# Batch 0 routed in two parts, two experts in TensorE's column halves, and gate logits out of the matmul that turns rows back

## The chip, the cores and the metric

The kernel runs on one core of one Trainium2 chip. The core has five engines with an instruction stream each: TensorE (PE in the rows; PEld is its weight load), VectorE (DVE), ScalarE (ACT), GpSimd (POOL) and SyncE (SP), which here only issues DMAs. The metric is the device time of one execution in microseconds (us), lower is better. One profiled execution stands behind all rows.

## The reference, cut to what matters

```python
# q, k, v: (4 batches, 8 heads, 576 tokens, 64)
scores = q @ k.T / sqrt(64)
kth    = the 32nd largest score of each row
attn   = softmax(scores where scores >= kth, else -1e9)
x      = (attn @ v), heads side by side          # (2304 tokens, 512)
noisy  = x @ w_gate + log1p(exp(x @ w_noise)) * noise   # (2304, 8 experts)
top2, weights = two largest of noisy, softmax over the two
out[t] = sum over the two experts: weight * (relu(x[t] @ w1[e]) @ w2[e])   # 512 -> 1024 -> 512
```

So there is a sparse attention whose thirty-second largest score must be found in each row, a gate that sends each token to two of eight experts, and the experts' two layers.

## The kernel before

**Attention** is done in 144 units of 128 score rows by 576 keys, 36 to a batch: four pairs of heads, nine units to a pair (`attend`, `finish`). For a unit PE makes the scores, DVE folds and searches them (`fold`, `top8`, `drop8`, lines 648 to 666), POOL subtracts the mask (line 739), ACT takes the exponential (line 687), PE turns the result (lines 762 and 766). After each fourth unit `gather` multiplies with the values (lines 824 to 836), lifts the product (849), turns it back into rows of tokens (`back`, line 853, a transpose against the identity `ident`) and writes it to the row buffer `xr` (`out_`, 859 and 861). DVE and POOL later divide by the softmax sums (`norm`).

**Gate.** Once a pair of heads is done, `gate` turns its 128 columns of all five token tiles again (lines 930 and 933), ACT copies them, and five matmuls with the gate weights `wg` (line 944) give the logits, which are summed over the four pairs. `route`, once a batch, makes the top two, the place of each token in its experts' lists, and ten indirect DMAs from POOL (`xg<-xr,si`, line 1125), which scatter the rows into the experts' slots `xg`.

**Experts** run in groups of slots (`experts`, table `GROUPS`): after batch 0 all eight experts take 128 slots each, after batches 1 and 2 come further groups, after batch 3 the last. In groups of 128 slots a piece is `up1` (eight float32 matmuls of 128 columns, line 1315) or half of `down1` (one of 512 columns, line 1342); four `up1` and eight halves make an expert. The groups of 256 slots split every number into a high and a low part and use three matmuls for one (lines 1284 to 1286 and 1350 to 1352). Gathered rows are first turned (line 1250). SP loads weights ahead (`wr`).

**Order.** Nothing is ordered by the engines at run time: `Plan` simulates the five engines when the program is built and writes each engine's instructions out in the order that its cost table and priorities (`prio`, `PACE`, `WHEN` and others) give. Each engine then runs its list strictly in order and waits by semaphore. Where PE would be idle before the first expert rows are turned, `Plan.fill` puts fillers in (`filler`, lines 572 to 576: matmuls whose result nobody reads). `qkv` loads the queries, keys and values of a head; SP issues its DMAs in list order too.

Of the kernel before, what the change touches and what calls it, by code (L numbers as in the profile page):

```python
# [34 lines left out]
SIGNS = (10, 10, 8, 5)  # L35


WEIGHS = (700, 2400, 2100, 3400)
BIAS = (2000, 500, 500, 500)
BELOW = (1100, -3100, 2200, 4500)  # L40
LOWK = (2300, 1900, 500, 2600)
OUTS = (300, -100, 300, 300)
NORM = (3000, 400, -100, -1700)
LOWS = (2100, 1600, 2700)
LOWN = 13


def spread(i, tenths):
# [6 lines left out]
LOADS = (3, 6)  # L55
# [10 lines left out]
DROPS = (4, 0, 2, 0)  # L66

TAKE = ((0, 208), (48, HS), (0, HS))
GLAG = 1

SGAP, SLOT = (1500, 1600, 1600, 1500), (1, 1, 1, 1)

WHEN = (16, 13, -21, -12)
# [7 lines left out]
NT = 5  # L81

NE2 = 4
# [4 lines left out]
PACE = [(70, 54), (910, 40), (110, 23), (300, 18), (0, 0)]  # L88


class Node:
    __slots__ = ("eng", "dur", "fn", "deps", "users", "prio", "left", "ready", "lat", "start", "n", "share", "move", "bank", "alt", "ready2", "shy", "lock", "gap")


class Plan:
# [13 lines left out]
    def add(self, eng, dur, fn, deps=(), prio=None, lat=0, share=1.0, move=0, bank=False, alt=None, lock=False, gap=None):  # L109
# [5 lines left out]
        x.shy, x.lock, x.gap = None, lock, gap  # L115
# [29 lines left out]
    def order(self):  # L145
# [13 lines left out]
        now = dict(free)  # L159

# [9 lines left out]
        while left:  # L170
# [21 lines left out]
            if x.lock:  # L192

                at = locked["DVE" if e == "POOL" else "POOL"]
                if at > t:
                    heapq.heappush(wait[e], (at, x.n, x))
                    continue
            if x.bank:
# [33 lines left out]
            if x.move:  # L232
                moved = end = max(end + 1000, moved) + x.move
            left -= 1
# [104 lines left out]
def general_path(tc, C, ident, qk, v, noise, w1, w2, out, dram):  # L339
# [5 lines left out]
    with ExitStack() as ctx:  # L345
# [57 lines left out]
        ps = ctx.enter_context(tc.tile_pool(name="gq", bufs=1, space=PSUM))  # L403
        with tc.For_i(0, N, 128) as r0:
# [11 lines left out]
            for c in range(4):  # L416
                nc.tensor.matmul(lg[:, 0], xt[:, c], C["wg"][:, c], start=(c == 0), stop=(c == 3))
# [32 lines left out]
def sparse_attention_moe(ctx: ExitStack, tc: tile.TileContext, qk, v, wg, aux, noise, w1, w2, out):  # L450
# [25 lines left out]
    ident = C["ident"] = cp.tile([128, 128], F32, name="ident")  # L476
    nc.vector.tensor_scalar(ident, jp, 0.0, None, op0=OP.is_equal)
    C["tri"] = cp.tile([128, 128], BF, name="tri")
# [10 lines left out]
    for b, lo, nt, es in GROUPS[:-1]:  # L489
        for e in es:  # L490
            ends.setdefault(("end", b), {})[e] = lo + 128 * nt
    for nm, at in ends.items():
        C[nm] = cp.tile([128, 8], F32, name=nm if isinstance(nm, str) else f"end{nm[1]}")
        e = 0
        while e < E:
# [3 lines left out]
            e += n  # L499
    zc = P["m"].tile([128, 2, XW], F32, name="xs", bufs=1)  # L500
# [14 lines left out]
    ENG = {"DVE": nc.vector, "POOL": nc.gpsimd}  # L515
    bank = P["acc"].tile([128, 512], F32, name="bank")
# [6 lines left out]
    QN = {}  # L523

    def qkv(n):
        b, h = divmod(n, H)

        def whole():
            hi[n] = P["hi"].tile([128, QW + KW], F32, name="hi", bufs=4)
            nc.sync.dma_start(hi[n][0:64], qk[b, h])  # L530
            vt[n] = P["v"].tile([128, 6, D], F32, name="vt", bufs=NV)
            nc.sync.dma_start(vt[n], v[b, h])

        if b < NATIVE:
            a = add("SP", 1000, whole, move=1330, lat=700)
            QN[n] = (a, a, a, pl.take("hi", 4, a), None, pl.take("v", NV, a))
            return

        def load():
# [3 lines left out]
            vt[n] = P["v"].tile([128, 6, D], F32, name="vt", bufs=NV)  # L543
            nc.sync.dma_start(vt[n], v[b, h])
# [13 lines left out]
        a = add("SP", 1500, load, move=2200, lat=2500)  # L558
        r, vv = pl.take("raw", 2, a), pl.take("v", NV, a)
# [4 lines left out]
        z = add("POOL", 1625, low_q, [x], alt=("DVE", 850, LOWK[b]), lock=True)  # L564
# [14 lines left out]
    def place(j):  # L579

        b, jj = divmod(j, 36)
        hp, tt = divmod(jj, 9)
# [952 lines left out]
```

## Time and profile before

| | us |
|---|---|
| median of 3 runs | 958.43 (958.23 to 958.78) |
| the profiled execution | 957.39 |
| its span, first to last instruction | 955.5 |

The span is 1.9 us shorter than the time of the same execution. The page counts PE as busy for 96% of the span, DVE for 70%, ACT, POOL for 69% each, with the TensorE clock granted at 0.99 of full speed in the mean. A busy PE is no proof that PE sets the end: the fillers count as busy too, and matmuls are pipelined, so that the mean duration of one matmul is longer than the distance from its start to the start of the next. The distance is what counts for a sum, and it is read from the timeline.

### The profile page before, as it was taken

To read this page: it belongs to the slowest core of one execution; us is meant where nothing else is said; L and a number is where in the kernel's file an instruction comes from. 1 tells how busy PE (TensorE), PEld (TensorE's weight loads), DVE (VectorE), ACT (ScalarE), POOL (GpSimd) and SP (SyncE) were. 2 spreads that over 40 slices of the span, in tenths; PEclk is the share of its full clock that TensorE was granted. 3 is DMA by queue.
4 is the path that set the end of the run, shared out by engine and by line. 5 is a ranking of instruction groups with operands and counts; after the bars stand their busy time and mean duration, and the time that the engine had idled before them with its cause. 6 is when DMAs were issued, how large, how long until landed. Compare 5 with 4: busy or idle time off the path is not lost.

```text
span 955.5 us, 18621 instructions
## 1 busy us (share of the span) xinstructions
PE 916.4 (96%) x6239; PEld 706.7 (74%) x6260; DVE 665.6 (70%) x2161; ACT 655.9 (69%) x1516; POOL 655.7 (69%) x840
## 2 busy tenths in 40 slices
PE   9999999999999899899999999999989999999992
PEld 4555566567777677777777877877889999999991
DVE  7999989998999999899998893773543222222220
ACT  4888888777987689788767675575556555555540
POOL 4666576873755787577687563249877988888871
PEclk9999999999999999999999999999999999999996
DMA  9364531236676677955959779567877787777731
GB/s 297 112 233 167 207 73 45 75 114 168 195 230 182 203 254 234 248 170 160 278 175 294 235 226 287 187 226 254 257 247 238 210 259 225 229 227 226 233 75 26
DMA packets 122251, 190.61 MB, mean 199 GB/s; under 512 B 8225, under 2 KB 69665, under 8 KB 122145
## 3 DMA queue, kind: packets, MB, share of 16 engines
q1 hardware_dynamic: 113440, 169.10, 55.6%
q0 software_dynamic: 8704, 20.22, 9.7%
q8 instruction: 51, 0.84, 0.4%
q14 instruction: 56, 0.45, 0.2%
HBM read 153.02 MB, written 36.27 MB: 198 GB/s over the span
## 4 chain that ended last, share of the span: by engine, by line
PE 76%; DMA 5%; POOL 5%; ACT 5%; DVE 4%; issue 3%; SPq 1%; POOLq 0%; DVEq 0%; ACTq 0%
PE bk L1342 9%; PE hps L1315 8%; PE pp L762 6%; PE bank L824 5%; PE hps L576 5%; PE bk L618 5%; PE hps L1284 5%; PE hps L1286 4%; PE hps L1285 4%; PE bk L614 4%; PE bk L1350 3%; PE bk L1351 3%; PE bk L1352 3%; DMA wr<-in_w_dram 2%; PE hps L1250 2%
## 5 line engine op out<-in xcount | busy, mean ns | idle before, releaser
L661 DVE MAX8 t8s<-cat 128x8 f32<-128x288 f32 (+3 forms) x576 | 265.7, 489 | 7.2 <-POOL cat L675 5.0
L739 POOL TENSOR_TENSOR ss<-ss,mk 128x576 f32<-128x576 f32 x143 | 186.0, 1304 | 76.8 <-ACT mk L729 60.5
L1200 POOL TENSOR_TENSOR wl<-wr,wh 128x1024 fp32r<-128x1024 f32 x77 | 188.1, 2479 | 33.7 <-ACT wh L1196 33.5
L666 DVE MATCH_REPLACE8 cat<-t8s,cat 128x240 f32<-128x240 f32 (+2 forms) x411 | 161.3, 395 | 0.0
L648 DVE TENSOR_TENSOR cat<-bk,ss 128x288 f32<-128x288 f32 x288 | 127.0, 444 | 27.8 <-ACT ss L626 27.7
L1294 DVE SCALAR_TENSOR_TENSOR hl<-hps,hh 128x256 fp32r<-128x256 f32 x96 | 40.6, 423 | 145.5 <-ACT hh L1290 134.2
L687 ACT ACTIVATE ss<-ss,nb 128x576 f32<-128x576 f32 x144 | 112.0, 778 | 27.5 <-POOL ss L739 21.6
L1196 ACT ACTIVATE wh<-wr 128x1024 fp32r<-128x1024 f32 x96 | 99.8, 1054 | 43.2 <-PE bk L1352 25.2
L1315 PEld LDWEIGHTS hps<-xh,wr 128*128 128x128 f32 x1024 | 120.7, 192 | 11.4 <-issue 5.0
L1315 PE MATMUL hps<-xh,wr 128*128 128x128 f32 x1024 | 125.2, 276 | 3.2 <-DMA wr<-in_w_dram 2.4
L1342 PE MATMUL bk<-wr,hh 128*128 128x512 f32 x256 | 127.2, 594 | 0.0
L626 ACT ACTIVATE ss<-bk 128x288 f32<-128x288 f32 x288 | 109.1, 412 | 22.9 <-PE bk L614 12.3
L1284 PE MATMUL hps<-xh,wh 128*128 128x256 f32 x384 | 111.1, 289 | 2.4 <-DVE hl L1294 2.4
L1286 PE MATMUL hps<-xh,wl 128*128 128x256 f32 x384 | 108.7, 283 | 0.4 <-POOL wl L1200 0.4
L1285 PE MATMUL hps<-xl,wh 128*128 128x256 f32 x384 | 108.5, 282 | 0.0
L729 ACT ACTIVATE mk<-ss,under 128x576 bf16<-128x576 f32 x118 | 91.5, 777 | 18.4 <-POOL under L725 13.7
L771 ACT ACTIVATE pt<-pp 128x512 f32<-128x512 f32 x144 | 86.1, 598 | 17.1 <-PE pp L762 16.0
L618 PE MATMUL bk<-hi 128*128 128x288 f32 x240 | 91.1, 389 | 2.9 <-POOL hi L556 1.3
L762 PE MATMUL pp<-ident,ss 128*128 128x128 f32 x576 | 89.5, 278 | 3.1 <-ACT ss L687 2.7
L762 PEld LDWEIGHTS pp<-ident,ss 128*128 128x128 f32 x576 | 66.2, 142 | 35.4 <-issue 10.2
L1370 POOL DMA_INDIRECT out_dram<-yo,tok x40 | 65.9, 1647 | 26.9 <-ACT yo L1366 16.5
L576 PE MATMUL hps<-dummy 128*128 128x512 bf16 x293 | 81.4, 388 | 2.0 <-DVE dummy L468 0.9
(159 smaller groups left out, 1901.7 us busy)
## 6 DMA issues: line engine op xcount, KB each, us to landing
wr<-in_w_dram SPq DMA_DIRECT2D x224, 512.0 KB
raw<-in_qk_dram SPq DMA_DIRECT2D x48, 320.0 KB
xg<-xs SPq DMA_DIRECT2D x16, 528.0 KB
xs<-xg SPq DMA_DIRECT2D x12, 528.0 KB
vt<-in_v_dram SPq DMA_DIRECT2D x32, 192.0 KB
out_dram<-xs SPq DMA_DIRECT2D x1, 5120.0 KB
xs<-xg SPq DMA_DIRECT2D x16, 264.0 KB
hi<-in_qk_dram SPq DMA_DIRECT2D x8, 320.0 KB
```

The costliest lines, as they stand in the source:

```text
L576: nc.tensor.matmul(ps, C["dummy"].to_broadcast([128, 128]), C["dummy"].to_broadcast([128, 512]), start=True, stop=True)
L618: nc.tensor.matmul(sp, lhs(n), rhs, start=(k == 0), stop=(k == 2 * len(heads) - 1))
L661: return lambda: nc.vector.max(t["t8"][:, r], t["cat"] if r == 3 else t["cat"][:, slice(*TAKE[r])])
L666: nc.vector.match_replace(g, t["t8"][:, r], g, NEG)
L739: ENG[eng].tensor_tensor(t["s"], t["s"], t["mk"], op=OP.subtract)
L762: nc.tensor.transpose(pp[:, c], t["s"][:, k0 + c * 128:k0 + (c + 1) * 128], ident)
L1200: return lambda eng: ENG[eng].tensor_tensor(WS[m][1][:, i], W[m][:, i], WS[m][0][:, i].bitcast(F32), op=OP.subtract)
L1284: nc.tensor.matmul(ps[:, :NN], ah, xh, start=(c == 0), stop=False)
L1285: nc.tensor.matmul(ps[:, :NN], ah, xl, start=False, stop=False)
L1286: nc.tensor.matmul(ps[:, :NN], al, xh, start=False, stop=(c == 3))
L1315: nc.tensor.matmul(ps[:, f * 128:(f + 1) * 128], w[:, 0, a:a + 128], X["h", e][:, c, :128], start=(c == 0), stop=(c == 3))
L1342: nc.tensor.matmul(Y[e][0], HN["h", ff // 2][:, f * 128:(f + 1) * 128], W[4 * e + ff // 2][:, 1, f * 512:(f + 1) * 512], start=(ff == 0), ...
```

## The change

Four things change.

1. **Batch 0 has two stages.** `STAGES` lists (batch, first tile, last tile). Stage 0 is token tiles 0 and 1 of batch 0, 16 units (four to a pair of heads); stage 1 is tiles 2 to 4, 20 units. Queries, keys and values of batch 0 are therefore loaded twice. Each stage is routed by itself: four scatters after stage 0 and six after stage 1 instead of ten after batch 0. The zero fills of `xg` and `out` move ahead (from every second unit to every unit, from unit 1 on), and the values of a head are loaded by a DMA of their own that comes later (`LATE`).
2. **Experts 0 and 1 go as a couple** (`couples`): 64 slots of expert 0 sit in partitions 0 to 63, 64 of expert 1 in 64 to 127, and each matmul uses one half of the array's columns. They do this once after stage 0 and once after stage 1, with their weights loaded each time (16 more weight DMAs of 0.5 MB in all). The group of 128 slots after batch 0 keeps experts 2 to 7. Fillers are now also allowed up to that group (`PH[2]` instead of `PH[0]`).
3. **No `gate` any more.** `back` is now a float32 matmul of 160 columns against `turn_gate`, which holds the identity and, beside it, this pair's gate weights, so that 32 of the columns are logits. `out_` copies rows and logits, two small pieces (`scale`, `gather_up`) scale and sum the logits, and one reduction on DVE ends them.
4. **The tables are set anew**: `SIGNS[0]` 8 instead of 10 (eight masks of batch 0 more on DVE, line 691, and eight less on ACT, line 729), `DROPS`, and the numbers that decide between DVE and POOL.

Counted over the program: PE loses 80 gate matmuls (line 944), 80 transposes of gate rows (930 and 933) and 25 fillers (314 to 289); 80 `back` transposes become 160-column matmuls; 64 of 512 `up1` matmuls and 16 of 128 `down1` matmuls go, 64 `up` and 32 `down` matmuls in column halves come.

```diff
+STAGES = [(0, 0, 2), (0, 2, NT), (1, 0, NT), (2, 0, NT), (3, 0, NT)]
+PAIRS, LATER = [(e, e + 1) for e in range(0, NP, 2)], range(8 - NE2, 8)
-GROUPS = [(0, 0, 1, range(8)), (1, 128, 1, range(8 - NE2, 8)), (2, 256, 1, range(8 - NE2, 8)), (2, 128, 2, range(8 - NE2)),
-          (3, 384, 2, range(8))]
+GROUPS = [(0, 0, 0, PAIRS), (1, 0, 1, range(NP, 8)), (1, 64, 0, PAIRS), (2, 128, 1, LATER), (3, 256, 1, LATER), (3, 128, 2, range(8 - NE2)),
+          (4, 384, 2, range(8))]
-SIGNS = (10, 10, 8, 5)
+SIGNS = (8, 10, 8, 5)
...
         if b < NATIVE:
-            a = add("SP", 1000, whole, move=1330, lat=700)
+            a = add("SP", 500, whole, move=800, lat=700)
+            VN[n] = add("SP", 500, values, move=530, lat=700, prio=pl.prio + LATE)
...
         def back():
             for k in range(nq):
-                nc.tensor.transpose(bank[:rows, 128 * k:128 * k + 128], t["ot"][:, k * 128:k * 128 + rows], ident)
+                nc.tensor.matmul(bank[:rows, 160 * k:160 * k + 160], t["ot"][:, k * 128:k * 128 + rows],
+                                 turn_gate[:, hp // 2, 32 * (hp % 2):32 * (hp % 2) + 160], start=True, stop=True)
...
+            l = (lp[:rows, 4:5] if rest else lp[:, 2 * u:2 * u + 2])[:, :, 1:].rearrange("p q i e -> p q (i e)")
+            for a, z in ((l, g), (o, x)):
+                if eng == "ACT":
+                    nc.scalar.activation(a, z, AF.Copy)
+                else:
+                    nc.vector.tensor_copy(a, z)
...
-    def gate(b, c):
...
-        for t in range(NT):
+        for t in range(t0, t1):
             for k in range(2):
...
+    def couples(gi):
...
+                for c in range(4):
+                    for i in range(2):
+                        nc.tensor.matmul(ps[64 * i:64 * i + 64], X["h", k][:, c, 64 * i:64 * i + 64], W[n, i][:, 0, c * 256:c * 256 + 256],
+                                         start=(c == 0), stop=(c == 3), skip_group_check=True)
...
+                for f in range(2):
+                    nc.tensor.transpose(ps[:, f * 128:f * 128 + 128], HN["q", n][:, f * 128:f * 128 + 128], ident)
...
+                for f in range(2):
+                    for i in range(2):
+                        nc.tensor.matmul(Y[k][64 * i:64 * i + 64], HN["h", n][:, f * 128 + 64 * i:f * 128 + 64 * i + 64],
+                                         W[n, i][:, 1, f * 512:(f + 1) * 512], start=(fp == 0 and f == 0), stop=(fp == 3 and f == 1),
+                                         skip_group_check=True)
...
-        FILLS.append(add("SP", 1500, fn, [T[4 + 2 * n]["note"]], move=3750 if n < E else 14600, lat=700))
+        FILLS.append(add("SP", 1500, fn, [T[1 + n]["note"]], move=3750 if n < E else 14600, lat=700))
...
-    pl.pauses = [(pl.nodes[0], PH[0]), (PH[-3], PH[-2])]
+    pl.pauses = [(pl.nodes[0], PH[2]), (PH[-3], PH[-2])]
```

How it moves instructions is shown at three places. The first is PE's list before, in the third pair of batch 0: turns of a unit (`pp<-ident,ss`), scores (`bk<-hi`) and fillers (`dummy`).

```order
L762 MATMUL pp<-ident,ss 128x128 x4
L614 MATMUL bk<-hi 128x288 x2
L766 MATMUL bank<-ident,ss 128x128
L762 MATMUL pp<-ident,ss 128x128 x4
L576 LDWEIGHTS dummy
L576 MATMUL hps<-dummy 128x512
```

At the same number of turned units PE's list of after has the couple's first pass: `wh` and `wl` are the weights of experts 0 and 1, line 1543 is `up`, 1582 `down`, 1553 the turn between them.

```order
L1543 MATMUL hps_1642<-wh_211,xh_1569 64x256
L1543 MATMUL hps_1642<-wl_214,xh_1569 64x256
L1582 MATMUL bk_1667<-wh_205,hl_1653 64x512
L1582 MATMUL bk_1667<-wl_208,hl_1653 64x512
...
L1553 MATMUL hps_1684<-turn_120,hh_1676 128x128 x2
L807 MATMUL pp_1696<-turn_120,ss_117 128x128 x4
L811 MATMUL bank_175<-turn_120,ss_117 128x128
L659 MATMUL bk_1705<-hi_1095 128x288
```

The couple's pieces stand between the units where fillers stood; the second pass stands between units 84 and 96, after batch 1 has been routed. The first gathered rows of the group after batch 0 are turned behind 51 turned units in PE's list before and behind 46 after; the last scatter of batch 0 stands behind 48 mask subtractions in POOL's list before and behind 44 after.

The second place is the end of a pair of heads on PE, before: the turn back of the last rows (853), the gate's turns (930, 933) and its matmuls (944).

```order
L853 MATMUL bank<-ident,ot 64x128
L930 MATMUL pp<-ident,xr 128x128 x4
L933 MATMUL bank<-ident,xr 128x128
...
L762 MATMUL pp<-ident,ss 128x128 x4
L766 MATMUL bank<-ident,ss 128x128
L944 MATMUL bank<-wg,pt 128x16 x5
```

After, at a gather of stage 0 (lines 872 and 876 are the values, 901 is `back`):

```order
L811 MATMUL bank<-turn,ss 128x128
L659 MATMUL bk<-hi 128x288 x2
L872 MATMUL bank<-pt,vt 64x256 x8
L876 MATMUL bank<-p_1006,vt 64x128
L876 MATMUL bank<-p_1075,vt 64x128
...
L807 MATMUL pp<-turn,ss 128x128 x4
L659 MATMUL bk<-hi 128x288 x2
L901 MATMUL bank<-turn,ot 128x160 x2
```

The gate's turns and matmuls are gone and nothing stands in their place but the wider `back`.

The third place is SP's list at the program's start, before: each head's values (`vt`) come right behind its queries and keys (`hi`), then the first weights.

```order
L914 DMA ax<-in_aux_dram 128x45
L530 DMA hi<-in_qk_dram 64x1280
L532 DMA vt<-in_v_dram 128x384
L530 DMA hi<-in_qk_dram 64x1280
L532 DMA vt<-in_v_dram 128x384
L914 DMA ax<-in_aux_dram 128x45
L1186 DMA wr<-in_w_dram 128x4x256
```

After, the values of the first four heads stand behind all early weights (`wh`, `wl` and `wr`, 14 DMAs of 0.5 MB) and behind the third pair's queries and keys:

```order
L1217 DMA wr<-in_w_dram 128x2x512
L575 DMA hi<-in_qk_dram 64x1280 x2
L579 DMA vt<-in_v_dram 128x384 x4
L1649 DMA xg<-xs 128x2x528 x2
L1649 DMA xg<-xs 128x528
```

The values moved behind the weights, and the zero fills (1649) follow them at once.

## Rows read from the trace of the kernel before

**Rows 1.** The page: busy time, share of the span, instructions.
```profile
PE 916.4 (96%) x6239; PEld 706.7 (74%) x6260; DVE 665.6 (70%) x2161; ACT 655.9 (69%) x1516; POOL 655.7 (69%) x840
```
**Rows 2.** Busy time: stretch, length, PE, PEld, DVE, ACT, POOL; PEclk, DMA share, GB/s.
```profile
10.00:215.00 205.00, 200.81 (x1245) 117.95 (x1265) 193.41 (x672) 167.66 (x410) 138.02 (x233) 1.00 0.44 145
215.00:500.00 285.00, 273.96 (x2045) 214.62 (x2044) 266.95 (x916) 229.08 (x585) 194.47 (x299) 1.00 0.70 207
500.00:640.00 140.00, 138.95 (x1014) 107.69 (x1012) 109.48 (x353) 92.20 (x239) 73.93 (x108) 1.00 0.79 244
700.00:938.00 238.00, 235.94 (x1524) 212.80 (x1522) 65.58 (x144) 130.49 (x217) 194.21 (x128) 1.00 0.71 209
```
**Rows 3.** Line 576, the fillers: ns min/median/max, first to last start.
```profile
L576 PE MATMUL hps<-dummy x293: 376/381/634, 0.9 to 211.5; 128*128 128x512 bf16 x147
```
**Rows 4.** PE's timeline from 205 us: start, us, line; first gathered rows turned.
```profile
214.91 0.38 PE L1250 MATMUL hps<-ident,xs 128*128 128x128 f32 x2
```
**Rows 5.** POOL's timeline, the first and the last of batch 0's ten scatters.
```profile
177.93 1.24 POOL L1125 DMA_INDIRECT xg<-xr,si  x1 [0.19 <-POOL spacer L1124]
...
206.40 0.92 POOL L1125 DMA_INDIRECT xg<-xr,si  x1 [0.18 <-issue]
```
**Rows 6.** DVE's groups from 0 to 215 us: shapes, count, busy us, mean ns.
```profile
L661 DVE MAX8 t8s<-cat 128x8 f32<-128x576 f32 x52 | 38.8, 749 | 3.1 <-POOL cat L675 2.9
...
L1067 DVE SCALAR_TENSOR_TENSOR tm<-c,away 128x10 f32<-128x10 f32 x1 | 1.3, 1308 | 0.0
L886 DVE RECIPROCAL rs<-sums 128x9 f32<-128x9 f32 x5 | 1.0, 204 | 0.1
```
**Rows 7.** DVE's groups of the whole span: the mask on DVE.
```profile
L691 DVE TENSOR_SCALAR mk<-ss,t8s 128x576 bf16<-128x576 f32 x26 | 14.8, 571 | 0.2
```
**Rows 8.** PE's timeline from 590 us: start, us, line; distances of starts are read.
```profile
592.96 1.95 PE L824 MATMUL bank<-pt,vt 128*64 128x256 f32 x16
594.74 0.61 PE L828 MATMUL bank<-p,vt 128*64 128x128 f32 x8
595.28 0.44 PE L1250 MATMUL hps<-ident,xs 128*128 128x128 f32 x2
...
596.85 0.38 PE L853 MATMUL bank<-ident,ot 128*128 128x128 f32 x2
597.07 0.60 PE L762 MATMUL pp<-ident,ss 128*128 128x128 f32 x4
...
605.95 0.60 PE L930 MATMUL pp<-ident,xr 128*128 128x128 f32 x4
...
606.42 0.38 PE L618 MATMUL bk<-hi 128*128 128x288 f32 x1
...
607.89 1.18 PE L944 MATMUL bank<-wg,pt 128*128 128x16 f32 x10
608.92 0.38 PE L618 MATMUL bk<-hi 128*128 128x288 f32 x1
...
616.05 1.88 PE L1342 MATMUL bk<-wr,hh 128*128 128x512 f32 x4
617.77 0.60 PE L762 MATMUL pp<-ident,ss 128*128 128x128 f32 x4
...
621.71 0.60 PE L762 MATMUL pp<-ident,ss 128*128 128x128 f32 x4
622.07 0.38 PE L618 MATMUL bk<-hi 128*128 128x288 f32 x1
...
622.67 1.02 PE L1342 MATMUL bk<-wr,hh 128*128 128x512 f32 x2
...
635.41 1.95 PE L1315 MATMUL hps<-xh,wr 128*128 128x128 f32 x16
637.20 0.27 PE L766 MATMUL bank<-ident,ss 128*128 128x128 f32 x1
```
**Rows 9.** Five early us, same columns as rows 2.
```profile
15.00:20.00 5.00, 4.68 (x19) 1.80 (x18) 4.66 (x19) 4.46 (x12) 3.40 (x7) 1.00 1.07 401
```

More of the change, by code (lines that the diff above doesn't have):

```diff
@@ L197, in order @@
                     continue
+            if x.drain and e == "POOL" and self.landed > t:
+                heapq.heappush(wait[e], (self.landed, x.n, x))
+                continue
             if x.bank:
@@ L522, in sparse_attention_moe @@
     raw, hi, kl, vt = {}, {}, {}, {}
-    QN = {}
+    QN, VN = {}, {}
+    UNITS = list(units())
+    VH = [(b, h) for b, _, _ in STAGES for h in range(H)]
     def qkv(n):
-        b, h = divmod(n, H)
+        b, h = VH[n]
         def whole():
@@ L563, in qkv @@
         kk = pl.take("kl", NK, y)
-        z = add("POOL", 1625, low_q, [x], alt=("DVE", 850, LOWK[b]), lock=True)
+        z = add("POOL", 1625, low_q, [x], alt=("DVE", 850, LOWK[b]), lock=True, drain=True)
         pl.give(r, y, z)
@@ L837, in few @@
                                      stop=(c == 4), skip_group_check=True)
-        av = add("PE", 735 if rest else 2315, few if rest else values, [x for m in pairs for x in PAIR[m]], share=0.5, bank=True)
+        av = add("PE", 735 if rest else 2315, few if rest else values, [x for m in pairs for x in PAIR[m]] + [VN[n0], VN[n0 + 1]], share=0.5, bank=True)
         for m in pairs:
@@ L870, in gather @@
+        if not done:
+            AVN["lp"] = []
+        AVN["lp"].append(pl.take(f"lp{2 if rest else u}", 1, q))
         done.append(q)
-        if len(done) < 3:
+        if len(done) < (t1 - t0 + 1) // 2:
             return
         for n in (n0, n0 + 1):
-            pl.give(QN[n][3], t["lastqk"])
+            qs = [x for i in T if (UNITS[i][0], UNITS[i][2]) == (st, hp) for x in T[i]["qk"]]
+            pl.give(QN[n][3], *qs)
             if QN[n][4]:
-                pl.give(QN[n][4], t["lastqk"])
+                pl.give(QN[n][4], *qs)
@@ L889, in norm @@
         def norm(eng):
[L890 to L896 removed]
+            n = tq - t0
@@ new lines, in gather_up, with logits @@
+        def gather_up():
+            l = lp[:, t0:t1]
+            nc.gpsimd.tensor_add(l[:, :, 0], l[:, :, 1 if hp == 0 else 0], l[:, :, 2])
+            if hp:
+                nc.gpsimd.tensor_add(l[:, :, 0], l[:, :, 0], l[:, :, 1])
+        def logits():
+            lgs[st] = P["xr"].tile([128, NT, 16], F32, name="lgs", bufs=1)[:, t0:t1]
+            nc.vector.tensor_reduce(lgs[st], lp[:, t0:t1].rearrange("p q i e -> p q e i"), axis=AX.X, op=OP.add)
+        m = add("POOL", 460, scale, [r] + done, alt=("DVE", 240, MULS[b]), lock=True, prio=pl.prio - (AHEAD if hp == 3 else 0))
@@ L904, in sparse_attention_moe @@
+        pl.give(br, m)
+        s = add("DVE", 330, logits, [m, AVN["lgn"]]) if hp == 3 else add("POOL", 316 if hp == 0 else 632, gather_up, [m, AVN.get("lgn")])
+        for p in AVN["lp"]:
+            pl.give(p, s)
+        AVN["lgn"] = s
+        if hp == 3:
+            AVN["lgn", st], AVN["lg", st] = s, pl.take("lgs", 1, s)
     lgs, axs, ROUTE, SENT, READ = {}, {}, {}, [], []
     def begin_batch(b):
-        def fn():
-            xr[b] = P["xr"].tile([128, NT, XW], F32, name="xr", bufs=2)
-            nc.gpsimd.memset(xr[b][:, :, DM:], 0.0)
-            nc.gpsimd.memset(xr[b][64:128, 4, :DM], 0.0)
+        xr[b] = rows[b % 2]
```

523 lines of the change are left out of this document (331 added, 192 removed).

## Prediction, made before the run

> **What bounds the kernel now.** I read three views, the stretches first. The page's shares [rows 1] mix stages: PE's 96% includes fillers, which run until 211.5 us [rows 3], and the first gathered rows are turned at 214.9 [rows 4]. So there are three stages [rows 2]. From 10 to 215 us DVE is busy for 193 of 205 us (94%): DVE sets the pace and PE is filled up. One full-width MAX8 goes to each unit; 52 of them by 215, with work from about 7 us on, make (215 - 7) / 52 = 4.0 us a unit [rows 6]. From 215 to 500 both are near their ends, PE 274 and DVE 267 of 285 us (96 and 94%). From 500 on PE alone is full (139 of 140, later 236 of 238) while DVE has slack. Once expert work has begun the kernel is PE's list played almost without a hole, so a gain has to make expert work begin earlier or leave PE less to do after it has begun.
>
> **Gate and turning back (PE).** A gate costs .47 us for its turns (605.95 to 606.42) and 1.03 for its matmuls (607.89 to 608.92), 1.5 in all [rows 8]. Eleven gates stand behind the first gathered rows in PE's list: -16.5. A `back` costs .11 now (596.85 to 597.07 for two). The new one has no row: 160 columns, not in transpose mode. The nearest is line 1315, eight float32 matmuls of 128 columns in 1.79, or .22; by columns that is .28. Ends are .22 and the .43 of 256 columns (half of line 1342's .86). With 54 of them after the start: 54 x (.28 - .11) = +9.2, ends +5.9 and +17.3. The copies of the logits and their sums go to ACT, DVE and POOL, where ACT loses a gate's three copies; only DVE's share is on a path, and only in the first stage (below).
>
> **Experts 0 and 1 (PE).** Now an expert of 128 slots is four times up (1.79) and down (1.72), plus four turns of .11: 14.5, two of them 29.0. A couple's up is eight matmuls of 256 columns in array halves. That is the shape of line 824: eight of them in 1.78 us (592.96 to 594.74), where one after the other they would take 8 x .43 = 3.44 [rows 8]. So halves do run side by side. Down has the same columns, 1.78; the turn between is .22. A pass: 4 x (1.78 + .22 + 1.78) + .44 = 15.6. The first pass goes into the stage where PE is filled up (fillers are its cover; without it, it costs 15.6), the second stays: 15.6 - 29.0 = -13.4. The two passes load 8.4 MB more of weights; the DMA share of that stage is 0.44 [rows 2].
>
> Line 824 shows pieces in halves between pieces of full width, at 1.78 where perfect overlap would be half of 3.44, 1.72: entering and leaving costs .06 a piece [rows 8]. The Trainium skill (TensorEngine Tiling (Array Packing), Key Properties) says that changing the tiling mode drains TensorE, which speaks against eight more pieces in halves; by this row that is 8 x .06 = .5 us, already in the 1.78, and the sum stays as it is; were each such drain as long as the .44 of a whole group of four turns, it would be 3.5 us worse.
>
> **When expert work begins.** It waits for the last scatter of batch 0, at 206.4 us, ten of them from 177.9 on [rows 5]. That scatter moves from behind 48 units to behind 44 in POOL's list: 4 x 4.0 = 16 us. Of those, PE spends its part on the four units' attention: scores .60 (622.07 to 622.67), turns .36 (621.71 to 622.07) plus .05, values 2.32 / 4 = .58 (592.96 to 595.28), about 1.65 a unit with `back` [rows 8], 6.6 in all. So 9.4 us are gained. PE's own list says five units (11.8), DVE's place lists two and a half (5.9): these are the ends.
>
> **What DVE gets in the first stage.** DVE sets the pace there, so each us is paid in full. Eight masks at .57 [rows 7]: 4.6. A second routing of fewer tiles: its costliest piece was 1.3 [rows 6], I take 3 for all. Four more reciprocals at .20, seven small copies at about the same: 2.2. Less is taken away than this rounds off. Sum about 9; ends 5 (pieces overlap) and 13 (routing at the full price).
>
> **The sum,** against the run's own 957.4 us: -16.5 + 9.2 - 13.4 - 9.4 + 9 = -21.1. From 215 to 500 DVE is nearly as full as PE, so I give 3 us back as holes that PE gets there: -18. That is 939.4; the median lies 1.0 above the profiled run, so I forecast **940**. After attention nothing else comes up: group-of-256 work covers the routing of batch 3 as before, and it is PE's list again.
>
> Added waits: behind the couple's first turn stand the next units' scores in PE's strict list. If slots or weights come late there, DVE lacks scores as soon as the three score banks are used up. And the first heads' values now stand behind 14 weight DMAs (7.3 MB), ten loads of queries and keys (3.3 MB); at 401 GB/s [rows 9] 26 us and the start-up, so they land near 32 us, where the fifth unit is done at 7 + 5 x 4 = 27. PE's gather then waits 5 us, but eight score buffers let DVE go on: 0, at worst 5.
>
> **Rivals.**
> 1. *DVE takes back what PE gives.* If from 215 to 500 us DVE's pace is the limit, PE's lighter list only gets holes there. PE has 11 us of holes now in that stretch, DVE 18. PE is relieved there of 13.4 us of expert work and of some 5 (seven gates less their wider `back`), against 6.6 of attention that begins earlier: 12 us. Then 12 us instead of 3 are lost: 949. For: 94% of DVE. Against: expert pieces can be pulled forward in the list, and from 500 to 640 us DVE is free for 31 of 140 us.
> 2. *Halves do not run side by side* for these operands: each piece 3.44 instead of 1.78, eight pieces on the path: +13, 953. Against: line 824.
> 3. *Slower: loads starve the first stage.* A pair of heads now feeds four or five units (16 to 20 us) where it fed nine (36), while zero fills (16 MB) and weights move into the same 60 us. A pair's load behind three fills (4 MB) waits 10 us at 401 GB/s. Five pairs, each late by L, cost 5 x L; above L = 3.6 the gain is gone, and at 6 us it is 30 - 18 = 12 above the median, 970. Against: each pair is loaded two pairs ahead, so a load has some 16 us.
> 4. *More is gained:* five units, `back` at .22, no holes: 940 - 2 - 3 - 3, and with DVE's additions at their low end 928.
> 5. *The change does not do what it says:* the couple's first pass slips behind the second stage (its slots wait for the fills). Then 15.6 us come back on the path: 956, hardly a gain.
>
> **Chances.** Forecast (932 to 946) 0.50; rival 1 (946 to 952) 0.20; rival 2 0.05; rival 3 0.08; rival 4 (below 932) 0.10; rival 5 and other ways to no change 0.04; slower for another reason 0.03. Faster by over 0.2% (1.9 us, about what a measurement can tell from no change): 0.50 + 0.20 + 0.05 + 0.10 = 0.85; same 0.04; slower 0.11. The range 928 to 955 leaves out rivals 3 and 5, the last 0.03 and a piece of rival 4: 0.19. It also takes in `back` at .43 with DVE's 13 (940 + 8 + 4 = 952).
>
> **What would show it.** In the profile after: couple pieces of 1.7 to 1.9 us for eight records pairs at some 115 to 150 us and again in batch 1; the first gathered rows of the group after batch 0 turned near 208 us (214.9 - 16 + 9); `back` at .25 to .3; no waits of DVE for scores before 100 us; PE at 96% from there to 500; DVE at 95% from 10 to the start. The forecast is wrong if expert work does not begin before 215, if PE waits for the couple's slots or weights by more than 5 us, or if holes of PE between the start and 500 us grow past 15.

## The result and the profile after

The changed kernel takes **947.71 us** (median of 4 runs, 946.95 to 948.84). The kernel before, on the same chip, took 958.61 (958.23 to 960.25). The ratio is 0.9866, its 95% interval 0.9817 to 0.9915: 10.9 us faster by the medians where 18 were forecast. (The two medians alone give 0.9886, inside that interval, so a figure below that is set against 0.9866 is uncertain by some 2 us.) The profiled execution took 947.64 us, its span is 945.4 (before 955.5).

The page of the changed kernel, as [rows 1]: busy time, share of the span, instructions.

```profile
PE 905.5 (96%) x6107; PEld 688.0 (73%) x6123; DVE 681.2 (72%) x2236; ACT 649.1 (69%) x1506; POOL 658.7 (70%) x875
```

Again the shares say little. The stretches of the changed kernel, in the columns of [rows 2], cut at the first gathered rows of the group that follows batch 0:

```profile
0.00:222.20 222.20, 206.96 (x1202) 118.34 (x1219) 182.26 (x650) 154.73 (x380) 148.42 (x281) 0.97 0.72 220
222.20:500.00 277.80, 271.66 (x2047) 206.82 (x2046) 268.59 (x959) 233.27 (x597) 205.88 (x307) 1.00 0.73 215
500.00:640.00 140.00, 137.61 (x975) 104.12 (x975) 124.19 (x403) 97.57 (x250) 76.61 (x112) 1.00 0.69 219
```

The first row holds the miss: PE idle for 15 of 222 us in a stage that has fillers, and DVE idle for 40. The second and third rows are as hoped, PE 98% busy. The first rows of that group are turned at 222.25 us, in the same view as [rows 4]; 208 was forecast, and before it was 214.91.

```profile
222.25 0.55 PE L1279 MATMUL hps<-turn,xs 128*128 128x128 f32 x2
```

What happened in the first stage stands in PE's timeline (start, us, line, in brackets the idle time and what ended it; a float32 matmul leaves two records):

```profile
28.19 2.35 PE L623 MATMUL hps<-dummy 128*128 128x512 bf16 x10
42.62 2.25 PE L659 MATMUL bk<-hi 64*128 64x288 f32 x4 [12.08 <-DMA hi<-in_qk_dram]
...
46.63 2.92 PE L872 MATMUL bank<-pt,vt 128*64 128x256 f32 x16
```

PE stands still for 12.08 us until the queries and keys of the third pair of heads have landed. DVE's longest wait is the same one, one step later (engine, tile and line, the engine waited for; us in all, times, longest):

```profile
DVE cat L693 <- ACT ss L671: 20.4, 6, 12.1
```

And this is why the load is late, in SP's timeline of issues:

```profile
25.76 0.37 SPq L1217 DMA_DIRECT2D wr<-in_w_dram  x1
27.22 0.37 SPq L1215 DMA_DIRECT2D wr<-in_w_dram  x1
28.42 1.37 SPq L1217 DMA_DIRECT2D wr<-in_w_dram  x1
29.90 1.26 SPq L575 DMA_DIRECT2D hi<-in_qk_dram  x2
31.22 4.29 SPq L579 DMA_DIRECT2D vt<-in_v_dram  x4
```

The load is issued at 29.90 and lands at 42.5, where PE goes on. From 4.78 to 29.8 us SP issued 18 loads ahead of it which nothing needs before 110 us: the couple's first weights (4.2 MB), raw queries and keys of batch 1 (1.3 MB), and weights of the group after batch 0 (3.1 MB). The slots that the load needs had been free since PE's sixteenth score record, at 10.9 us: of the 31.6 us from there to the landing, 19.0 pass before the issue and 12.6 behind it.

The end moved less than the start. From the first turned rows to POOL's last issue of an indirect DMA to the output it is 939.20 - 214.91 = 724.3 us before and 933.92 - 222.25 = 711.7 after; the tail behind that issue is 16.3 and 11.5. Together: +7.3 at the start, -12.6 in the list, -4.8 in the tail, -10.1 of span.

### The profile page after: what moved, and what is told of

The parts are those of the page before. It is cut to its first block, busy times and chain, and to the rows that moved or that the text cites. A ratio compares the mean times of both kernels' runs of the same rounds, so it can differ in the third digit from the quotient of the medians.

```text
span 945.4 us, 18475 instructions
## 1 busy us (share of the span) xinstructions
PE 905.5 (96%) x6107; PEld 688.0 (73%) x6123; DVE 681.2 (72%) x2236; ACT 649.1 (69%) x1506; POOL 658.7 (70%) x875
## 3 DMA queue, kind: packets, MB, share of 16 engines
q0 software_dynamic: 8992, 20.75, 10.1%
## 4 chain that ended last, share of the span: by engine, by line
PE 83%; DMA 4%; DVE 4%; POOL 3%; SPq 2%; ACT 1%; issue 1%; POOLq 0%; DVEq 0%; ACTq 0%
PE hps L1344 9%; PE bk L1371 9%; PE pp L807 6%; PE bk L663 6%; PE bank L872 6%; PE hps L623 5%; PE hps L1315 5%; PE hps L1313 5%; PE hps L1314 4%; PE bk L659 4%; PE bk L1379 3%; PE bk L1381 3%; PE bk L1380 3%; PE bank L901 3%; PE hps L1279 2%; PE y L1379 2%
## 5 line engine op out<-in xcount | busy, mean ns | idle before, releaser
L1229 POOL TENSOR_TENSOR wl<-wr,wh 128x1024 fp32r<-128x1024 f32 x67 | 165.7, 2491 | 41.3 <-ACT wh L1225 30.3
L1371 PE MATMUL bk<-wr,hh 128*128 128x512 f32 x224 | 111.4, 594 | 0.0
L1344 PE MATMUL hps<-xh,wr 128*128 128x128 f32 x896 | 109.5, 275 | 0.0
L1344 PEld LDWEIGHTS hps<-xh,wr 128*128 128x128 f32 x896 | 105.7, 192 | 4.4 <-issue 4.3
L774 ACT ACTIVATE mk<-ss,under 128x576 bf16<-128x576 f32 x110 | 85.5, 778 | 14.8 <-POOL under L770 11.6
L807 PE MATMUL pp<-turn,ss 128*128 128x128 f32 x576 | 90.0, 279 | 2.5 <-ACT ss L732 1.2
L807 PEld LDWEIGHTS pp<-turn,ss 128*128 128x128 f32 x576 | 66.4, 141 | 35.2 <-issue 12.4
L1399 POOL DMA_INDIRECT out_dram<-yo,tok x38 | 62.0, 1630 | 23.2 <-ACT yo L1395 12.6
L623 PE MATMUL hps<-dummy 128*128 128x512 bf16 x273 | 73.8, 391 | 2.0 <-DVE dummy L494 0.9
```

The lines of the kernel that those rows point to most:

```text
L807: nc.tensor.transpose(pp[:, c], t["s"][:, k0 + c * 128:k0 + (c + 1) * 128], ident)
L1229: return lambda eng: ENG[eng].tensor_tensor(WS[m][1][:, i], W[m][:, i], WS[m][0][:, i].bitcast(F32), op=OP.subtract)
L1344: nc.tensor.matmul(ps[:, f * 128:(f + 1) * 128], w[:, 0, a:a + 128], X["h", e][:, c, :128], start=(c == 0), stop=(c == 3))
L1371: nc.tensor.matmul(Y[e][0], HN["h", ff // 2][:, f * 128:(f + 1) * 128], W[4 * e + ff // 2][:, 1, f * 512:(f + 1) * 512], start=(ff == 0), ...
```

## The experiments

Times are medians beside runs of the kernel before on the same chip. "Start" is the first turned rows of the group after batch 0, "list" the time from there to POOL's last issue to the output; both are from the profiled execution. There is one such execution for each run, and the times of one kernel lie up to 5.5 us apart; those of "heads first" (950.06) and "third pair later" (958.98) are the longest of their kernels.

| run | us | before | ratio (95%) | start | list | longest wait of PE before the start |
|---|---|---|---|---|---|---|
| changed kernel | 947.71 | 958.61 | 0.9866 (0.9817 to 0.9915) | 222.25 | 711.7 | 12.1, third pair's queries and keys |
| third pair first | 946.32 | 957.14 | 0.9865 (0.9823 to 0.9906) | 218.62 | 714.2 | 7.8, first values |
| heads first | 948.15 | 957.14 | 0.9878 (0.9833 to 0.9923) | 218.54 | 717.6 | 8.2, values of the fourth pair |
| third pair later | 954.62 | 957.14 | 0.9958 (0.9912 to 1.0005) | 228.24 | 715.9 | 17.1, third pair's queries and keys |
| all by need | 945.87 | 958.03 | 0.9873 (0.9840 to 0.9905) | 216.09 | 714.4 | 6.5, the couple's rows |
| by need, weights last | 936.27 | 957.35 | 0.9772 (0.9749 to 0.9796) | 208.44 | 715.5 | 0.9 |
| thin first pass | 946.58 | 957.35 | 0.9886 (0.9859 to 0.9913) | 216.64 | 715.2 | 10.2, third pair's queries and keys |
| a gate's work back on PE | 967.73 | 958.03 | 1.0093 (1.0059 to 1.0128) | 221.93 | 731.6 | 11.5, third pair's queries and keys |
| turning back twice | 962.09 | 954.79 | 1.0073 (1.0049 to 1.0097) | 220.98 | 726.0 | 10.6, third pair's queries and keys |
| gate alone | 967.90 | 957.14 | 1.0083 (1.0038 to 1.0128) | 217.96 | 733.2 | 3.0, copies of scores on ACT |
| gate alone, loads in order | 960.49 | 954.79 | 1.0053 (1.0036 to 1.0070) | 207.18 | 736.1 | 0.9 |

### The order of the loads

Theory: SP's order starves the first stage, and the wait is paid at the end. Rivals: the stage lacks DMA time whatever the order; or what is saved at the start comes back behind it. Five runs move loads on SP's queue and nothing else; the order on PE, DVE, ACT and POOL stays that of the changed kernel. The edit is this, with a list of moves (written here with short names for the loads):

```diff
+    seq = pl.order()
+    for late, first in MOVES:                  # nodes, and the node behind which they go
+        seq = [x for x in seq if x not in late]
+        at = seq.index(first) + 1
+        seq[at:at] = late
     with tc.manual_schedule():
-        for x in pl.order():
+        for x in seq:
             x.fn()
```

Below, `WH` are the couple's two early weight loads, `WR` the three early ones of the next group, `RAW` the two raw loads of batch 1; `QN[n][0]` and `VN[n]` load queries and keys, and values, of a head.

**Third pair first:**

```diff
+    MOVES = [(WR, QN[5][0]), (RAW, QN[5][0])]
```

> Edit: on SP's queue alone, the raw loads of batch 1 and three early weights of the next group (4.5 MB) go from just ahead of the third pair's queries and keys to just behind them; the couple's first weights stay ahead, and all that comes later has the same bytes ahead of it as in the changed kernel. Theory (each load lands when the bytes ahead of it are through, and values and the fourth pair have the same bytes ahead as before): the third pair lands near 26 us and its wait of 12.1 us goes, but PE then waits about as long for the values of the first pair (landing near 44, wanted near 33) or for the fourth pair, whose wait is 6 to 12 us; time 942 to 948. Rival (the third pair's place alone matters): 934 to 937.

**Heads first:**

```diff
+    MOVES = [(WR, QN[9][0]), (RAW, QN[9][0]), (WH, QN[7][0])]
```

> Edit: on SP's queue alone, the two early couple weight loads stand behind the load of head 7, the raw loads of batch 1 and three early weights of the next group behind head 9; the order on PE and DVE is as in the changed kernel. Theory (SP's order starves the first stage: the third pair's queries and keys landed at 42.48 us behind 8.6 MB that nothing needs before 120 us, PE and DVE stood still for 12.1 us, and the clock granted behind it cost 2 more): no wait of PE for a load over 2 us before 100 us, first gathered rows of the next group turned at 207 to 210 instead of 222.2, time 933 to 937. Rival A (the first stage is short of DMA time as a whole, busy share 1.05 from 10 to 95 us, so the wait comes up again at a later pair, at the scatters or at the couple's weights): turned at 217 or later, time 943 to 948. Rival B (DVE takes it back behind the start): turned at 208 but holes of PE behind it larger by 8, time 942.

**Third pair later:**

```diff
+    MOVES = [([QN[4][0], QN[5][0]], FILLS[1])]
```

> Edit: on SP's queue alone, the third pair's queries and keys go behind four loads of values and the first two zero fills, 3.4 MB more. Theory (the wait of PE in the first stage is paid in full at the end): landing 10 to 13 us later than 42.48, PE's wait 22 to 25 instead of 12.1, time 957 to 961. Rival (the wait is covered by slack that DVE has elsewhere in the first stage, 83% busy from 10 to 208): the wait grows as much but the time by less than half of it, 948 to 953.

PE's longest wait before the start, in the order of these three runs, as the view of the waits has it (one fence for each kernel):

```profile
PE bank L874 <- DMA vt<-in_v_dram: 7.8, 1, 7.8
```

```profile
PE bank L874 <- DMA vt<-in_v_dram: 8.2, 1, 8.2
```

```profile
PE bk L661 <- DMA hi<-in_qk_dram: 17.1, 1, 17.1
```

With the third pair first, the 12.1 us are gone and 7.8 us of waiting for the first values have come in their place, as the theory had it: those have the same bytes ahead of them as in the changed kernel, and the time is the same (ratio 0.9865 against 0.9866). With the third pair later the wait is 5.0 longer, which is half of what I had expected, and start and time follow it: start 6.0 later in the profiled execution, the median 6.9 us longer, the ratio up by 0.0092, some 9 us. 954.62 lies between the theory's range and the rival's. The five more us of waiting are paid in full, with 7 to 9, though the two intervals just touch. The other way it is not seen yet: with the third pair first the start is 3.6 us earlier and the time the same.

Heads first did not do what the theory promised (933 to 937; it took 948.15, with the start at 218.54, which is what rival A had forecast). My order was bad: raw loads and weights, 4.5 MB, now stood ahead of the fourth pair's values. From this run alone the rival that the stage lacks DMA time as such could not be put aside. So the next run orders all loads by the time at which they are wanted:

```diff
+    MOVES = [(WH, QN[11][0]), ([FILLS[-1]], VN[11]), (RAW, FILLS[-1]), (WR, VN[13])]
```

> Edit: on SP's queue alone, loads stand by the time at which they are wanted: the couple's two early weight loads behind head 11's load, the zero fill of the output and then batch 1's raw loads behind the values of head 11, the next group's early weights behind the values of head 13. The run with heads first moved the weights only part of the way: PE then waited 8.2 us for the values of the fourth pair, which stood behind 4.5 MB of raw loads and weights and three fills. Theory (it is the order of the loads, not the amount): no wait of PE for a load over 2 us before 110 us, next group's first rows turned at 207 to 211 instead of 222.2, time 932 to 938. Rival (the first stage lacks DMA time as such: 22 MB before the first scatter): a wait of 6 us or more comes up at another pair, time 943 to 949.

No load is late before 110 us any more, but then one is:

```profile
PE hps L1525 <- DMA xs<-xg: 6.5, 1, 6.5
```

These are the couple's gathered rows. Their load was issued at 108.62 right behind the 3.1 MB of `WR`. The start, 216.09, missed my 207 to 211, and the wait of 6.5 and the time of 945.87 are what the rival had forecast; against it speaks only that the wait fell on the couple's rows and not on a pair of heads. The last move puts `WR` where SP's queue has room:

```diff
-    MOVES = [..., (WR, VN[13])]
+    MOVES = [..., (WR, QN[21][0])]
```

> Edit: as in the run with all loads by need, and the three early weight loads of the next group (3.1 MB) stand behind the raw loads of head 5 of batch 1 instead of ahead of the couple's rows; there PE had waited 6.5 us for these rows. Theory (the end follows the start of the next group one to one: 723 to 729 us from its first turned rows to the span's end in five runs): no wait for the couple's rows over 2 us, first rows turned at 207 to 210 (216.1 less 6.5, and less up to 2 for the clock behind the wait), span 931 to 938, time 933 to 940. Rival (what is saved at the start comes back behind it, as it partly did: start 6.2 earlier, span 2.3 shorter): start 208, span 939 to 942, time 941 to 944.

**936.27 us**, ratio 0.9772 (0.9749 to 0.9796): 9 us faster than the changed kernel by the ratios, 11 by the medians, and the fastest here. Start, span (935.4) and time lie in the theory's ranges. Its stretches, columns as in [rows 2]:

```profile
30.00:50.00 20.00, 20.00 (x120) 11.48 (x119) 18.53 (x61) 15.51 (x39) 12.41 (x25) 1.00 0.88 297
50.00:70.00 20.00, 20.00 (x104) 11.17 (x104) 18.24 (x63) 16.01 (x40) 13.87 (x28) 1.00 1.06 328
70.00:90.00 20.00, 20.00 (x104) 11.19 (x102) 19.07 (x68) 15.41 (x40) 14.65 (x33) 1.00 0.89 302
90.00:110.00 20.00, 19.98 (x146) 11.48 (x145) 18.77 (x69) 14.41 (x41) 17.21 (x36) 1.00 0.93 293
```

and the first turned rows in its PE timeline:

```profile
208.44 0.55 PE L1282 MATMUL hps<-turn,xs 128*128 128x128 f32 x2
```

From 30 to 110 us PE is never without work (fillers count as work), with nearly the same bytes moved: 297 GB/s from 10 to 110 us, 29.7 MB, where the changed kernel moved 30.8 MB. `WR` now goes at 172 us, 36 us before it is wanted. The stage does not lack DMA time; the order was at fault.

What is saved at the start does not come back step by step either: over the changed kernel and these five, the start lies anywhere from 208.4 to 228.2, while the list stays at 711.7 to 717.6, with 715.5 behind the earliest start and 715.9 behind the latest. The changed kernel's own 711.7 is the shortest, and the end of the runs with a start near 218 is for that reason hardly earlier than its own. The traces show where this difference lies: some 500 us behind the start PE waits for gathered rows of the last group, 0.8 us in the changed kernel, 4.7 with heads first and 1.7 to 3.7 in the other four.

```profile
PE hps L1279 <- DMA xs<-xg: 0.8, 1, 0.8
```

```profile
PE hps L1282 <- DMA xs<-xg: 4.7, 1, 4.7
```

In each of these five, too, the granted clock was .66 to .91 in the mean of one or two stretches of 5 us between 460 and 520 us behind the start, where the changed kernel had 1.00 throughout. What makes that wait longer or shorter stays open.

### What the couple's first pass costs

```diff
-                for c in range(4):
+                for c in range(4 if gi else 1):
...
-                for f in range(2):
+                for f in range(2 if gi else 1):
```

> Edit: the changed kernel with the couple's first pass thinned: two of its eight matmuls in each up piece and two of four in each down piece (the same for both array halves), so 6/8 of 1.87 and 1/2 of 1.82 us, 2.3 us in each of four steps, 9.2 us of TensorE's work is left out of the part from 125 to 165 us; the rows that this pass gives are not those of the reference. Prediction's step (the pass costs nothing there, since fillers cover it): within 2 us of 947.7. Rival (between 130 and 165 us PE is full with 1.4 us of fillers in 35, and DVE, at 74%, waits for PE there): 6 to 9 us faster, 939 to 942, and DVE at 85% or more between 130 and 165.

From 125 to 165 us, in the columns of [rows 2], first the changed kernel and then the thinned one:

```profile
125.00:165.00 40.00, 39.77 (x242) 21.85 (x243) 31.21 (x103) 30.76 (x74) 28.74 (x45) 1.00 0.71 208
```

```profile
125.00:165.00 40.00, 35.84 (x232) 20.22 (x231) 32.13 (x107) 33.42 (x84) 31.67 (x49) 1.00 0.81 255
```

PE gets 4 us of holes there and DVE is 80% busy instead of 78%: taking 9 us of work off PE hardly makes DVE faster. The time is that of the changed kernel (0.9886 against 0.9866, 946.58 against 947.71), so the rival's 6 to 9 us fall, and so does its DVE at 85%. That the pass costs nothing at all isn't shown: the start at 216.64 is 5.6 earlier, of which 2 are a shorter wait for the third pair in this execution (10.2), and the list that gives the other 3.6 back is as long (715.2) as in runs that leave the pass alone. So up to some 4 us of start may be its price. What holds DVE at 78 to 80% in this stretch (it was 38 of 40 us before) isn't settled.

### The prices of a gate and of turning back

```diff
+    def again():
+        for _ in range(7):
+            nc.tensor.matmul(bank[:, 496:512], ident, turn_gate[:, 0, 32:48], start=True, stop=True)
...
             x.fn()
+            if x in LAST[8:]:      # the last out_ of a head pair, batches 1 to 3
+                again()
```

> Edit: in the changed kernel, behind the last turn back of each of the 12 head pairs of batches 1 to 3, PE gets 7 more float32 matmuls of 16 columns into unused columns of the bank, which nothing reads; a gate of the kernel before was five such in 1.03 us and .47 of turns, so 7 are 1.44, the PE time of a gate. All else stays. Theory (behind the start PE's list is played without a hole, so a gate's PE time is paid in full, as the term of -16.5 has it): 12 x 1.44 = 17 slower, 963 to 967 against 947.7. Rival (until 500 us DVE's pace or other waits have slack in which a gate hides): half of it or less, 951 to 957.

967.73, ratio 1.0093 against 0.9866. In PE's timeline the seven matmuls (14 records) take 303.19 to 304.75, 1.56 us:

```profile
303.19 1.63 PE L1707 MATMUL bank<-turn 128*128 128x16 f32 x14
304.75 0.69 PE L887 MATMUL bank<-pt,vt 128*64 128x64 f32 x16
```

Twelve of them are 19; the list is 731.6, 17 above the mean of the six kernels with the same lists (714.9), the time 20 longer. A gate's PE time put in behind the start was paid in full, and the rival, that it hides in DVE's pace up to 500 us, falls. That a gate taken away is gained in full follows only if the rest of the list stays as it is; the last section of the experiments shows a case where it did not.

```diff
-            for k in range(nq):
-                nc.tensor.matmul(bank[:rows, 160 * k:160 * k + 160], ...)
+            for k in range(nq):
+                for _ in range(2 if b else 1):
+                    nc.tensor.matmul(bank[:rows, 160 * k:160 * k + 160], ...)
```

> Edit: the changed kernel with each float32 matmul of 160 columns that turns rows back issued twice in batches 1 to 3 (60 more of them, the same result written again). It prices the term +9.2 of the prediction (54 x (.28 - .11)). By the .28 of the prediction: 60 x .28 = 17 slower, 964 to 966 against 947.7. By the changed kernel's rows (two in .65, .33 each): 20 slower, 966 to 969. Rival (a waiting PE has room for them, or the second of two with the same weights costs only its columns, .22 or less): 13 or less, at most 961.

PE's timeline of the changed kernel and of this run, a pair of tiles each; distances of starts are read:

```profile
263.42 0.71 PE L901 MATMUL bank<-turn,ot 128*128 128x160 f32 x4
263.97 0.60 PE L807 MATMUL pp<-turn,ss 128*128 128x128 f32 x4
```

```profile
262.81 1.25 PE L904 MATMUL bank<-turn,ot 128*128 128x160 f32 x8
263.90 0.60 PE L809 MATMUL pp<-turn,ss 128*128 128x128 f32 x4
```

Two take .55, four 1.09: .27 each. (The .33 that I quoted in the expectation came from 149.15 us, between pieces in column halves.) Sixty are 16 by the rows; the list grew by 11, the time by 14 as it stands (962.09, just below my 964 and above the rival's 961) and by 20 when put against the kernel before on the same chip. The price lies between .19 and .33, with the rows in the middle.

### The gate part alone

Of the change the logits in `back` are kept, with one stage for batch 0, eight ordinary experts and the planner's numbers of the kernel before. Two smaller parts of the change stay in as well, which the expectation below does not list: the zero fills that move ahead, and the values' own, later DMA (`LATE`).

```diff
-SIGNS = (8, 10, 8, 5)
+SIGNS = (10, 10, 8, 5)
...
-STAGES = [(0, 0, 2), (0, 2, NT), (1, 0, NT), (2, 0, NT), (3, 0, NT)]
+STAGES = [(0, 0, NT), (1, 0, NT), (2, 0, NT), (3, 0, NT)]
...
+GROUPS = [(0, 0, 1, range(8)), (1, 128, 1, LATER), (2, 256, 1, LATER), (2, 128, 2, range(8 - NE2)),
+          (3, 384, 2, range(8))]
```

> Edit: batch 0 in one part again, eight ordinary experts in its group and the planner's numbers of the kernel before; of the change only the gate logits in the matmul that turns rows back are left. By the prediction's terms: gates -16.5, wider back +9.2, copies and sums off the path: 951 against 958.6. With back at the .33 us that the changed kernel shows instead of .28: 54 x .05 = 3 more, 954. Rival (the extra copies, sums and multiplies on ACT, DVE and POOL take the rest back in the first stage, where DVE sets the pace): 957 to 960, first gathered rows turned later than 214.9.

It is slower, 967.90 against 957.14, beyond my 951 to 954 and beyond the rival's range too, and its start at 217.96 is 3.1 later than before. Part of that is an order of loads again: GpSimd waited 7.0 us for the noise load (`ax`), which stood behind raw loads. Hence a second run with those loads later:

```diff
+    MOVES = [(WR, FILLS[1]), (RAW, FILLS[-1])]
```

> Edit: as in the run with the gate alone (batch 0 in one part, ordinary experts), with the early weights of the next group behind the first two zero fills and batch 1's raw loads behind the last. There the noise load stood behind 1.3 MB of raw loads, GpSimd waited 7.0 us for it and held back what stood behind it, PE stood still for 3 us near 16 us and TensorE's clock was granted at half level from 20 to 30 us; a second stretch at .66 lay at 660 to 670. Theory (the gate part is worth what its PE terms say, and that run lost 10 to 15 us by the order of loads and of PE's list): first stage as in the kernel before or up to 3 later, time 950 to 957. Rival (the gate part alone is worth nothing or costs: its copies, sums and multiplies hold up ACT, POOL and DVE): 960 to 968.

960.49 against 954.79: still 0.5% slower, above my 950 to 957 and in the rival's 960 to 968, though its start is at 207.18, 7.7 earlier than before. The loss is in the list, 736.1 instead of 724.3, where the prediction's two terms would make it 7.3 shorter. Two stretches of it, in the columns of [rows 2]:

```profile
300.00:400.00 100.00, 94.33 (x663) 73.78 (x662) 91.18 (x313) 74.84 (x194) 72.86 (x122) 0.95 0.71 213
...
640.00:680.00 40.00, 35.13 (x227) 29.51 (x226) 17.42 (x43) 17.37 (x32) 28.53 (x30) 0.91 0.63 208
```

PE has holes here (5.7 and 4.9 us; in the kernel before 3.3 and 1.1) and the clock was granted at .95 and .91 in the mean, where the kernel before was at 1.00 in both. By these shares the two stretches would be some 8.6 us shorter at full clock (an estimate: .05 x 100 + .09 x 40). So most of the loss is holes and clock, not PE's work, and the gate part is no gain by itself in a list laid out with the old numbers. Whether it is one in a list laid out for it stays open: these runs can't tell the edit from its layout.

## Why the prediction was right, and where it failed

The sign and the range (928 to 955) held; the size, 940, was missed by 7.7 us. The way there was in part luck. By the prediction's own sign (wrong "if expert work does not begin before 215") its forecast of the start had failed: the start was to come 6.9 us earlier and came 7.3 later. The list made up for it, 12.6 us shorter where 11.1 were forecast, and so did the tail, 4.8 us shorter, for which the prediction had no term. By its steps:

- **What bounds the kernel: right.** Expert work sets the end once it has begun: six starts over a range of 20 us leave the list within 6 us.
- **Gate, -16.5: borne out from the other side.** The PE time of twelve gates put back cost 17 us of list and 20 of time. Taken away by itself, the gate brought nothing in the two runs above, in a list with more holes.
- **Back, +9.2: right within one and a half.** Behind the start the tiles that are turned in twos take .27 each where .28 was taken, but the 12 single ones of 64 rows take .42, which the prediction did not tell apart: 42 x .16 + 12 x .31 = 10.4. The profile has the single ones in a column half (128*64):

```profile
224.50 0.49 PE L901 MATMUL bank<-turn,ot 128*64 128x160 f32 x2
224.92 2.05 PE L1344 MATMUL hps<-xh,wr 128*128 128x128 f32 x16
```

- **Couples, -13.4: right by the rows, not tried by itself.** A piece takes 1.76 to 1.88 us where 1.78 was taken, .3 us more over the eight pieces of a pass. No run takes the couples out of the list. PE's timeline, the first rows of an up piece and what follows it:

```profile
128.12 0.43 PE L1543 MATMUL hps<-wh,xh 128*64 128x256 f32 x1
128.12 0.43 PE L1543 MATMUL hps<-wl,xh 128*64 128x256 f32 x1
128.38 0.38 PE L1543 MATMUL hps<-wh,xh 128*64 128x256 f32 x1
128.39 0.38 PE L1543 MATMUL hps<-wl,xh 128*64 128x256 f32 x1
...
129.99 0.51 PE L659 MATMUL bk<-hi 64*128 64x288 f32 x1
```

  The two experts' matmuls start within .01 of each other: rival 2 falls. The first pass costs at most some 4 us of start. What entering and leaving costs can be read from the neighbours of a piece: 1.87 with full-width work on both sides (128.12 to 129.99, and a down piece 138.41 to 140.28), 1.82 with halves before it (134.52 to 136.34), 1.78 and 1.76 with halves behind it (132.74 to 134.52, 152.17 to 153.93). Against the 1.72 of perfect overlap, both together cost .15, more than the .06 that line 824 showed and far from the .44 that I had held against it:

```profile
138.41 0.64 PE L1582 MATMUL bk<-wh,hl 128*64 128x512 f32 x1
...
140.28 0.66 PE L807 MATMUL pp<-turn,ss 128*128 128x128 f32 x4
```

  This agrees with the drain between tiling modes of which the Trainium skill speaks (TensorEngine Tiling (Array Packing), Key Properties), though no run here separates a drain from other causes of the .15.
- **Attention moved behind the start, +6.6, and holes, +3:** together with the three terms above the list was to be 11.1 shorter. It is 12.6 shorter in the changed kernel and 6.7 to 10.1 in the runs that only move loads. PE is idle for 6.1 us from 222 to 500 where it was idle for 11.0 from 215 to 500, so the 3 us of holes never came: rival 1 falls. These terms were checked only in this sum.
- **DVE's +9: too high.** The groups of DVE up to the start hold eight masks at .52 (4.1 us) and 2.6 us more of copies from the bank; the second routing has no piece over .8 and one reduction takes the place of the old sum. That is about 7. But DVE is also busy 6.7 us less from 125 to 165 than before, a loss that I had not listed.
- **The start at 208: this step failed,** and it is rival 3's mechanism that broke it. The step is the sentence "Against: each pair is loaded two pairs ahead, so a load has some 16 us". That looks at the slots, which were free at 10.9 us; but a load also has to get past what SP issued before. I had counted just that for the values ("behind 14 weight DMAs (7.3 MB)", landing near 32) and found it harmless there, and did not ask the same of the third pair's queries and keys, in the same queue at the same place. I also took 401 GB/s; it was 310 from 10 to 30 us. One wait of 12.1, not five of 6, with the clock behind it (below), is the 14 us by which the start was late. When the loads stand in order it comes at 208.44. That it then meets the forecast of 208 to half a microsecond is luck in part, as DVE's two misses go opposite ways.
- **The rest:** with the start where it was forecast, the time is 936.3, below 940. The tail behind POOL's last issue is 11.5 in that run and 16.3 in the profiled execution of before, and the prediction had them equal. It goes with the couples or the new tables, not with the gate part: it is 11.2 to 12.9 in all nine kernels that have them and 15.5 to 16.3 in the three that don't. Why stays open.

Of the signs that I named, the couple's pieces, the price of `back` (in twos) and PE's share after the start came as said; the first turned rows and "no waits of DVE for scores before 100 us" did not, and they pointed at the step that failed. DVE at 95% from 10 us to the start did not come either: it was 83% from 10 to 208 us in the changed kernel and 90% with the loads in order.

## What to carry to other kernels

When a change loads more, or loads earlier, follow each load that is wanted soon through its queue: count the bytes issued ahead of it, not only the slot that it waits for, and do so for every load in that place. Eighteen loads that nobody needed for 100 us cost 9 to 11 us here because they were issued first. A wait taken away shows the next one in the same queue: three of the four orders tried for it left one other load late, behind 3 MB or more, and brought 4 to 6 us at the start and nothing that the time showed.

## What the runs showed of the hardware

In these runs a stop of PE cost more than its length: with a wait of 12.1 us the start came 13.8 us later than with the loads in order. In the changed kernel PE stood still from 30.5 to 42.6 us, and the clock was granted at half its level (0.50, the 1.2 of 2.4 GHz) from 35 us on and for some us behind the stop; columns as in [rows 2]:

```profile
30.00:35.00 5.00, 0.54 (x3) 0.04 (x1) 3.22 (x10) 1.81 (x4) 3.54 (x7) 1.00 1.08 366
35.00:40.00 5.00, 0.00 (x0) 0.00 (x0) 0.00 (x0) 0.00 (x0) 0.00 (x0) 0.50 1.06 242
40.00:45.00 5.00, 2.38 (x5) 1.29 (x6) 0.00 (x0) 0.50 (x2) 0.00 (x0) 0.50 1.05 334
45.00:50.00 5.00, 5.00 (x31) 3.01 (x30) 2.90 (x10) 2.34 (x5) 1.47 (x2) 0.64 1.08 381
```

The eight value matmuls (sixteen records) at 46.63 took 2.75 us to the next start, 1.78 at full clock [rows 8]. In the first of the two runs with the gate alone, a stop of 2.96 us that ended at 18.6 us was followed by some 15 us at half level, although PE was busy for all but .6 us of the 15 from 20 on:

```profile
15.00:20.00 5.00, 1.92 (x4) 0.60 (x3) 2.97 (x12) 1.43 (x3) 2.18 (x5) 0.76 1.08 327
20.00:25.00 5.00, 4.43 (x11) 1.94 (x12) 1.79 (x6) 3.67 (x11) 2.33 (x4) 0.50 1.06 371
25.00:30.00 5.00, 5.00 (x13) 2.03 (x12) 4.77 (x15) 1.77 (x6) 0.70 (x3) 0.50 1.06 386
30.00:35.00 5.00, 5.00 (x12) 1.80 (x13) 2.57 (x11) 2.80 (x7) 3.54 (x7) 0.53 0.68 245
```

What kept the clock down for so long there stays open.
